# Moving the steps of a softmax in a fused FFT and mixture-of-experts kernel: normalisation, transposition and input rounding

## The chip, the cores and the metric

The kernel runs on one core of one Trainium2 chip. The metric is the device time of one execution in microseconds (us). An execution of the kernel before took 1669.15 us in the median of three (1666.14 to 1671.22).

## The reference

The input is x with 8 batches of 3072 x 256. What is computed, cut to what matters:

```
X = fft(fft(x, axis=1), axis=2).real          # 8 x 3072 x 256, then 24576 rows of 256
x = (X @ w_a * (X @ w_b)) @ w_out             # 256 -> 1536 -> 256
logits = x @ phi                              # 24576 x 32
d = softmax of logits over the 24576 rows     # one column for each of 32 slots
slot_input = d.T @ x                          # 32 x 256, 8 experts of 4 slots
slot_out = per expert relu(slot_input @ w1) @ w2
c = softmax of logits over the 32 slots       # one row for each of 24576 rows
out = c @ slot_out
```

All of it is single precision. Both softmaxes subtract the maximum, and add 1e-9 to the sum that they divide by.

## The kernel before, in words

**Three stages.** `_fft` makes the transform in the first 214 us of the profiled execution. `_main` runs the loop over 24 blocks of rows, three for each batch, and ends with `tail`, which computes the slots. `_out` writes the result in the last 65 us.

**The loop.** A block k has 12 steps p, one for each 128 of the 1536 hidden columns (n = 12 k + p). The order of each engine's instructions is the order in which the program writes them; nothing reorders them. In a step:

- `layer1(n)`: TensorE makes 12 products of 512 columns into four PSUM tiles s0, s1, d0, d1, each of one buffer. VectorE adds and subtracts them (L547 twice, then L552, L553, L554), ScalarE copies d1 (L551, `db`), and GpSimd makes the products `g` of the two layers with three instructions that read and write SBUF (L556, L557, L558). In every third block (k % 3 = 2) GpSimd also copies one column (L561). The next step's s products can't start before L547 has read s, nor its d products before L552, L553 and L554 have read d.
- `transp(n - 2)`: eight transpositions of `g` by TensorE (L579) and a copy of them by ScalarE into a ring (L582).
- at p = 1, 5 and 9: `logits` of four steps (L590, 32 products).
- `run_side(k - 1, ...)`: the softmax of the block before, by the list `side`, and with p = 5, 9 and the next block's 1 the product `z_part` (L599, 16 products) with its sum into `acc` (L602).

**The softmax of a block** has the parts `l` and `m` (p = 1: copy of the logits, maximum, exponential `dt` L620), `d` (p = 3), `ct` (p = 4, transposition), `cm` (row maximum L643, subtraction L644, exponential L645), `sum` (the sum of `dt`, L625, and the running sum L626), `cs` (the normalisation: sum L650 on VectorE, plus eps L651 on ScalarE, reciprocal L652 and product L653 on VectorE) and `co` (two transpositions L658, copy L660, store to DRAM by SyncE's queue L661). The list before is

```
side = {3: ["d"], 4: ["ct"], 5: ["cm", "sum", 0], 9: ["cs", 1], 10: ["co"]}
```

**The next block's inputs** are loaded by `load_eo(k + 1)`, written at p = 1, into one buffer `eoraw`. `split_eo(k + 1)` at p = 9, written right behind `layer1`, rounds them to `eoh` on ScalarE (L516) and takes the rest `eol` as a difference on VectorE (L519), an instruction with two inputs in SBUF. Both tiles have two buffers.

Of the kernel before, what the change touches and what calls it, by code (L numbers as in the profile page):

```python
# [10 lines left out]
F32R = mybir.dt.float32r  # L11
U32 = mybir.dt.uint32
U64 = mybir.dt.uint64
ACTF = mybir.ActivationFunctionType
ALU = mybir.AluOpType
AX = mybir.AxisListType
# [3 lines left out]
P = 128  # L20
# [467 lines left out]
def _main(tc, ctx, wtp, wt, w128, outs, eo, wsc, exu, ident, m_sb, ex_e, csc, nblk, wof, w1, w2):  # L488
    nc = tc.nc
    nb = nblk // 3  # L490
    ep = ctx.enter_context(tc.tile_pool(reuse_waits="tile", name="m_e", bufs=2))
    eh = ctx.enter_context(tc.tile_pool(reuse_waits="tile", name="m_h", bufs=2))
# [9 lines left out]
    eo_t = {}  # L502

    def load_eo(k):
        raw = ep.tile([P, 2, 512], F32, tag="eoraw", name="eoraw", bufs=1)
        ub = ep.tile([P, 512], F32, tag="ub", name="ub")
        nc.sync.dma_start(raw, eo[k])
        nc.sync.dma_start(ub, eo[k][0:1, 1, :].to_broadcast([P, 512]))
        eo_t[k] = [raw, ub]

    def split_eo(k):
        raw, ub = eo_t[k]
        l = eh.tile([P, 2, 512], F32R, tag="eol", name="eol")
        h = eh.tile([P, 2, 512], F32R, tag="eoh", name="eoh")
        if k:
            nc.scalar.copy(h, raw)  # L516
        else:
            nc.vector.tensor_copy(h, raw)
        nc.vector.tensor_tensor(l, raw, h.bitcast(F32), ALU.subtract)  # L519
        eo_t[k] = (h, l, ub)  # L520

    load_eo(0)
    split_eo(0)
    nper = nblk * NFT
    g_t = {}
    r_t = {}
# [57 lines left out]
    def logits(n):  # L584
        k, ft = divmod(n, NFT)
        g = g_t[n] if n == nper - 1 else g_t.pop(n)
        if ft == 0:
            l_ps[k] = ps.tile([P, 256], F32, tag="l", name="l_ps")
        for c in range(4):
            nc.tensor.matmul(l_ps[k][NS * c:NS * c + NS], m_sb[:, ft], g[:, 256 * c:256 * c + 256],  # L590
                             start=(ft == 0), stop=(ft == NFT - 1))

    def z_part(k, q, tag="x"):
        z_ps = ps.tile([P, 512], F32, tag=tag, name="z_ps")
        d_sb, alpha = soft[k]["d"], soft[k]["alpha"]
        ring = r_t.pop((k, q))
        for hh in range(2):
            for c in range(4):
                nc.tensor.matmul(z_ps[NS * c:NS * c + NS], d_sb[:, hh, NS * c:NS * c + NS],  # L599
                                 ring[:, :, 2 * c + hh, :], start=(hh == 0), stop=(hh == 1))  # L600
        sl = acc[:, q * 512:q * 512 + 512]
        nc.vector.scalar_tensor_tensor(out=sl, in0=sl, scalar=alpha, in1=z_ps,  # L602
                                       op0=ALU.mult, op1=ALU.add)

    def soft_step(k, step):
        s = soft.setdefault(k, {})
        if step == "l":
            l_sb = p2.tile([P, 256], F32, tag="l_sb", bufs=1, name="l_sb")
            (nc.scalar.copy if k < nblk - 1 else nc.vector.tensor_copy)(l_sb, l_ps.pop(k))
            s["l"] = l_sb  # L610
        elif step == "m":
            l_sb = s["l"]
            m_old, m_new = m_run[k % 2], m_run[1 - k % 2]
            bm = p2.tile([P, 4], F32, tag="sm", name="sm")
            dt_ = p2.tile([P, 256], F32, tag="dt", bufs=1, name="dt")
            nc.vector.tensor_reduce(out=bm[:, 0:1], in_=l_sb, axis=AX.X, op=ALU.max)
            nc.vector.tensor_tensor(m_new, bm[:, 0:1], m_old, ALU.max)
            nc.vector.tensor_scalar_mul(bm[:, 1:2], m_new, -1.0)
            al = p2.tile([P, 2], F32, tag="al", name="al")
            nc.scalar.activation(dt_, l_sb, ACTF.Exp, bias=bm[:, 1:2])  # L620
            nc.scalar.activation(al[:, 0:1], m_old, ACTF.Exp, bias=bm[:, 1:2])
            s["dt"], s["alpha"], s["al"] = dt_, al[:, 0:1], al
        elif step == "sum":
            al = s["al"]
            nc.vector.tensor_reduce(out=al[:, 1:2], in_=s["dt"], axis=AX.X, op=ALU.add)  # L625
            nc.scalar.activation(l_run, l_run, ACTF.Identity, scale=al[:, 0:1], bias=al[:, 1:2])  # L626
        elif step == "d":
            y_ps = ps.tile([P, 2, P], F32, tag="x", name="y_ps")
            for hh in range(2):
                nc.tensor.transpose(y_ps[:, hh], s["dt"][:, hh * P:hh * P + P], ident)  # L630
            d_sb = p2.tile([P, 2, P], F32, tag="d_sb", bufs=1, name="d_sb")
            nc.scalar.copy(d_sb, y_ps)
            s["d"] = d_sb
        elif step == "ct":
            x_ps = ps.tile([P, 4, P], F32, tag="x", name="x_ps")
            for hh in range(2):
                nc.tensor.transpose(x_ps[:, hh], s["l"][:, hh * P:hh * P + P], ident)
            s["xl"] = x_ps
        elif step == "cm":
            x_ps = s.pop("xl")[:, 0:2].rearrange("p h (c s) -> p (h c) s", c=4)  # L640
            cm = p1.tile([P, 8], F32, tag="cm", name="cm")
            ce = p1.tile([P, 8, NS], F32, tag="ce", name="ce")
            nc.vector.tensor_reduce(out=cm, in_=x_ps, axis=AX.X, op=ALU.max)  # L643
            nc.vector.tensor_tensor(ce, x_ps, cm.unsqueeze(2).to_broadcast([P, 8, NS]), ALU.subtract)  # L644
            nc.scalar.activation(ce, ce, ACTF.Exp)  # L645
            s["ce"] = ce
        elif step == "cs":
            ce = s["ce"]
            cs = p1.tile([P, 8], F32, tag="cs", name="cs")
            nc.vector.tensor_reduce(out=cs, in_=ce, axis=AX.X, op=ALU.add)  # L650
            nc.scalar.activation(cs, cs, ACTF.Identity, bias=eps)  # L651
            nc.vector.reciprocal(out=cs, in_=cs)  # L652
            nc.vector.tensor_tensor(ce, ce, cs.unsqueeze(2).to_broadcast([P, 8, NS]), ALU.mult)  # L653
        elif step == "co":
            x_ps = ps.tile([P, 2, P], F32, tag="x", name="c_ps")
            cf = s["ce"].rearrange("p a s -> p (a s)")
            for hh in range(2):
                nc.tensor.transpose(x_ps[:, hh], cf[:, hh * P:hh * P + P], ident)  # L658
            ct = p2.tile([P, 256], F32, tag="ct", bufs=1, name="ct")
            nc.scalar.copy(ct, x_ps.rearrange("p h t -> p (h t)"))  # L660
            nc.sync.dma_start(csc[:, k], ct)  # L661

    side = {3: ["d"], 4: ["ct"], 5: ["cm", "sum", 0], 9: ["cs", 1], 10: ["co"]}

    def run_side(k, items):
        for v in items:
            if isinstance(v, str):
                soft_step(k, v)
            else:
                z_part(k, v)  # L670

    ex = {}
# [62 lines left out]
    def tail(k, rest):  # L735
        load_w1(2)
        soft_step(k, "m")
        rest()
        soft_step(k, "sum")
        load_w2(0)  # L740
        soft_step(k, "d")
# [120 lines left out]
    for z in range(4):  # L862
        nc.vector.tensor_reduce(out=fold[:, z], in_=ident.rearrange("p (c s) -> p s c", c=4),
                                axis=AX.X, op=ALU.add)
# [4 lines left out]
    for n in range(nper + 2):  # L869
        k, p = divmod(n, NFT)  # L870
        if n < nper:
            if p == 1 and k + 1 < nblk:
                load_eo(k + 1)
            layer1(n)
            if p == 9 and k + 1 < nblk:
                split_eo(k + 1)
            if n < 9:
                extra(n)
            if n == NFT:
                nc.sync.dma_start(wo, wof)  # L880
        if n == nper + 1:
            for z in range(5, 1, -1):
                logits(n - z)
        if n >= 2:
            rest = transp(n - 2)
        if n == nper:
            z_part(nblk - 2, 2)
        if n % 4 == 1 and 1 < n < nper:
            for z in range(5, 1, -1):
                logits(n - z)  # L890
        if k > 0 and p == 1:
            soft_step(k - 1, "l")
            if n < nper:
                soft_step(k - 1, "m")
                if k > 1:
                    z_part(k - 2, 2)
        if k > 0 and n < nper:
            run_side(k - 1, side.get(p, []))
        if k == nblk - 1 and p in ahead:
            ahead[p]()  # L900
# [40 lines left out]
def _build(tc, x, x384, w_a, w_b, w_out, phi, w1, w2, tabs, fdft, out):  # L941
# [3 lines left out]
    with ExitStack() as ctx, tc.manual_schedule():  # L945
# [45 lines left out]
        with ExitStack() as c1:  # L991
            cin, first, so_h, so_l = _main(tc, c1, wtp, wt, w128, outs, eo, wsc, exu, ident, m_sb, ex_e, csc,
                                    nblk, wof, w1, w2)
# [36 lines left out]
```

## Time and profile before

| | us |
|---|---|
| three executions: lowest, median, highest | 1666.14, 1669.15, 1671.22 |
| the profiled execution | 1664.62 |
| its span, from the first to the last instruction | 1662.6 |
| busy in the span: TensorE (PE) | 1598.5 (96%) |
| VectorE (DVE) | 1391.2 (84%) |
| GpSimd (POOL) | 1146.9 (69%) |
| ScalarE (ACT) | 640.8 (39%) |
| mean granted clock of TensorE | 0.98 of its upper level |

The profiled execution is a run of its own, 4.5 us below the median. PE, DVE, ACT and POOL are the engines' names in the profile; PEld is TensorE's weight load and SPq SyncE's queue of transfers. Matmuls overlap, so that the time from the start of one to the start of the next is a better measure than its duration.

### The profile page before, as it was taken

To read this page: it belongs to the slowest core of one execution; us is meant where nothing else is said; L and a number is where in the kernel's file an instruction comes from. 1 tells how busy PE (TensorE), PEld (TensorE's weight loads), DVE (VectorE), ACT (ScalarE), POOL (GpSimd) and SP (SyncE) were. 2 spreads that over 40 slices of the span, in tenths; PEclk is the share of its full clock that TensorE was granted. 3 is DMA by queue.
4 is the path that set the end of the run, shared out by engine and by line. 5 is a ranking of instruction groups with operands and counts; after the bars stand their busy time and mean duration, and the time that the engine had idled before them with its cause. 6 is when DMAs were issued, how large, how long until landed. Compare 5 with 4: busy or idle time off the path is not lost.

```text
span 1662.6 us, 28294 instructions
## 1 busy us (share of the span) xinstructions
PE 1598.5 (96%) x10837; PEld 1166.9 (70%) x10837; DVE 1391.2 (84%) x2055; ACT 640.8 (39%) x990; POOL 1146.9 (69%) x992
## 2 busy tenths in 40 slices
PE   5999999999999999999999999999999999999985
PEld 3555578777777777777777777777777777777554
DVE  8999889888888888888888988888888888888633
ACT  1322324434434444434343443433443434434343
POOL 1000069888878887888788778877887788878421
PEclk9999999999999999999999999999999999999975
DMA  9777330000000000000000000000000000002689
GB/s 392 271 249 243 106 98 20 23 1 23 24 23 1 23 23 23 1 23 23 23 1 23 23 20 4 23 23 16 8 23 23 1 23 23 23 1 94 281 338 385
DMA packets 34095, 123.71 MB, mean 74 GB/s; under 512 B 3780, under 2 KB 12035, under 8 KB 26792
## 3 DMA queue, kind: packets, MB, share of 16 engines
q1 hardware_dynamic: 28796, 113.98, 18.7%
q10 hardware_dynamic: 5164, 7.92, 1.3%
q8 instruction: 86, 1.41, 0.4%
q14 instruction: 49, 0.40, 0.1%
HBM read 79.36 MB, written 42.52 MB: 73 GB/s over the span
## 4 chain that ended last, share of the span: by engine, by line
PE 81%; DVE 11%; DMA 4%; issue 2%; ACT 1%; POOL 0%; DVEq 0%; ACTq 0%; SPq 0%
PE t_ps L579 14%; PE s L531 8%; PE d L531 8%; PE d L533 8%; PE d L532 8%; PE s L533 7%; PE s L532 7%; PE l_ps L590 7%; PE z_ps L599 6%; PE pt L262 4%; DMA out_dram<-o 3%; DVE eol L519 2%; PE pt L171 1%; DVE f L269 1%; DVE e L276 1%
## 5 line engine op out<-in xcount | busy, mean ns | idle before, releaser
L556 POOL TENSOR_TENSOR db<-s_sb,db 128x512 f32<-128x512 f32 x287 | 373.0, 1300 | 249.7 <-DVE s_sb L553 99.1
L547 DVE SCALAR_TENSOR_TENSOR s_sb<-ub,w,s 128x512 f32<-128x512 f32 x576 | 404.4, 743 | 72.0 <-PE s L533 69.8
L551 ACT COPY db<-d 128x512 f32<-128x512 f32 x288 | 169.7, 589 | 626.7 <-PE d L533 608.7
L557 POOL TENSOR_TENSOR g<-pl 128x512 f32<-128x512 f32 x288 | 384.9, 1336 | 7.7 <-DVE pl L554 6.9
L558 POOL TENSOR_TENSOR g<-s_sb,db 128x512 f32<-128x512 f32 x287 | 372.4, 1298 | 0.0
L582 ACT COPY ring<-t_ps 128x1024 f32<-128x1024 f32 x286 | 290.5, 1016 | 63.8 <-PE t_ps L579 63.8
L579 PE MATMUL t_ps<-ident,g 128*128 128x128 f32 x2296 | 297.3, 272 | 0.0
L579 PEld LDWEIGHTS t_ps<-ident,g 128*128 128x128 f32 x2296 | 268.3, 140 | 39.3 <-issue 0.4
L531 PE MATMUL s<-eoh,wt 128*128 128x512 f32 x576 | 252.6, 438 | 2.4 <-DVE s_sb L547 2.4
L531 PE MATMUL d<-eoh,wt 128*128 128x512 f32 x576 | 226.9, 394 | 3.1 <-DVE s_sb L553 3.1
L533 PE MATMUL d<-eoh,wt 128*128 128x512 f32 x576 | 227.2, 394 | 0.0
L533 PE MATMUL s<-eoh,wt 128*128 128x512 f32 x576 | 226.5, 393 | 0.0
L532 PE MATMUL s<-eol,wt 128*128 128x512 f32 x576 | 225.2, 391 | 0.0
L532 PE MATMUL d<-eol,wt 128*128 128x512 f32 x576 | 225.1, 391 | 0.0
L553 DVE TENSOR_TENSOR s_sb<-s_sb,d 128x512 f32<-128x512 f32 x288 | 197.8, 687 | 9.9
L554 DVE TENSOR_TENSOR pl<-s_sb,d 128x512 f32<-128x512 f32 x288 | 197.5, 686 | 0.5 <-ACT db L551 0.5
L552 DVE TENSOR_TENSOR pl<-s_sb,d 128x512 f32<-128x512 f32 x288 | 195.6, 679 | 0.0
L531 PEld LDWEIGHTS s<-eoh,wt 128*128 128x128 f32 x576 | 108.4, 188 | 76.1 <-issue 28.9
L590 PE MATMUL l_ps<-g,m_sb 128*32 128x256 f32 x2304 | 139.2, 382 | 0.0
L599 PE MATMUL z_ps<-ring,d_sb 128*32 128x512 f32 x1152 | 136.7, 592 | 0.0
L531 PEld LDWEIGHTS d<-eoh,wt 128*128 128x128 f32 x576 | 108.2, 188 | 30.7 <-DVE s_sb L553 7.6
L533 PEld LDWEIGHTS s<-eoh,wt 128*128 128x128 f32 x576 | 108.1, 188 | 25.0
(186 smaller groups left out, 1699.5 us busy)
## 6 DMA issues: line engine op xcount, KB each, us to landing
out_dram<-o SPq DMA_DIRECT2D x23, 1024.0 KB
xt<-in_x_dram SPq DMA_DIRECT2D x15, 1536.0 KB
eoraw<-eo_c SPq DMA_DIRECT2D x16, 512.0 KB
w2t<-in_moe_w_dram SPq DMA_DIRECT2D x4, 2048.0 KB
w1t<-in_moe_w_dram SPq DMA_DIRECT2D x3, 2048.0 KB
eo<-so SPq DMA_DIRECT2D x16, 256.0 KB
eoraw<-eo SPq DMA_DIRECT2D x8, 512.0 KB
ub<-eo_c SPq DMA_DIRECT2D x16, 256.0 KB
```

The costliest lines, as they stand in the source:

```text
L531: nc.tensor.matmul(ps_, wt[ft // 4][:, ft % 4, 0, e, ab], h[:, e], start=True, stop=False)
L532: nc.tensor.matmul(ps_, wt[ft // 4][:, ft % 4, 0, e, ab], l[:, e], start=False, stop=False)
L533: nc.tensor.matmul(ps_, wt[ft // 4][:, ft % 4, 1, e, ab], h[:, e], start=False, stop=True)
L547: nc.vector.scalar_tensor_tensor(out=s_sb[:, ab], in0=ub, scalar=w128[:, ab, ft:ft + 1], in1=s_ps[ab], op0=ALU.mult, op1=ALU.add)
L553: nc.vector.tensor_tensor(am, s_sb[:, 0], d_ps[0], ALU.subtract)
L556: eng.tensor_tensor(bm, s_sb[:, 1], db, ALU.subtract)
L557: nc.gpsimd.tensor_tensor(g[:, 0:512], pl[:, 0], pl[:, 1], ALU.mult)
L558: eng.tensor_tensor(g[:, 512:1024], am, bm, ALU.mult)
L579: nc.tensor.transpose(t_ps[:, z], g[:, z * P:z * P + P], ident)
L582: nc.scalar.copy(dst, t_ps)
L590: nc.tensor.matmul(l_ps[k][NS * c:NS * c + NS], m_sb[:, ft], g[:, 256 * c:256 * c + 256], start=(ft == 0), stop=(ft == NFT - 1))
L599: nc.tensor.matmul(z_ps[NS * c:NS * c + NS], d_sb[:, hh, NS * c:NS * c + NS], ring[:, :, 2 * c + hh, :], start=(hh == 0), stop=(hh == 1))
```

## The change

`split_eo` becomes two functions, `split_h` (the rounding) and `split_l` (the difference), which `run_side` calls at p = 8 and p = 9, behind the step's transpositions. The normalisation `cs` goes from p = 9 to p = 5, behind `sum` and ahead of the first `z_part`, and `co` from p = 10 to p = 7. The reduction L625 is taken out: the exponential L620 gives its sum by `accum_out`. `run_side` is now called in block 0 too, for the two new steps alone.

```diff
-    def split_eo(k):
-        raw, ub = eo_t[k]
+    def split_h(k):
+        h = eh.tile([P, 2, 512], F32R, tag="eoh", name="eoh")
+        (nc.scalar.copy if k else nc.vector.tensor_copy)(h, eo_t[k][0])
+        eo_t[k].append(h)
+
+    def split_l(k):
+        raw, ub, h = eo_t[k]
         l = eh.tile([P, 2, 512], F32R, tag="eol", name="eol")
-        h = eh.tile([P, 2, 512], F32R, tag="eoh", name="eoh")
-        if k:
-            nc.scalar.copy(h, raw)
-        else:
-            nc.vector.tensor_copy(h, raw)
         nc.vector.tensor_tensor(l, raw, h.bitcast(F32), ALU.subtract)
         eo_t[k] = (h, l, ub)
 
     load_eo(0)
-    split_eo(0)
+    split_h(0)
+    split_l(0)
...
-            nc.scalar.activation(dt_, l_sb, ACTF.Exp, bias=bm[:, 1:2])
+            nc.scalar.activation(dt_, l_sb, ACTF.Exp, bias=bm[:, 1:2], accum_out=al[:, 1:2])
...
             al = s["al"]
-            nc.vector.tensor_reduce(out=al[:, 1:2], in_=s["dt"], axis=AX.X, op=ALU.add)
...
-    side = {3: ["d"], 4: ["ct"], 5: ["cm", "sum", 0], 9: ["cs", 1], 10: ["co"]}
+    side = {3: ["d"], 4: ["ct"], 5: ["cm", "sum", "cs", 0], 7: ["co"], 8: ["h"], 9: ["l", 1]}
 
     def run_side(k, items):
+
         for v in items:
-            if isinstance(v, str):
+            if v in ("h", "l"):
+                if k + 2 < nblk:
+                    (split_h if v == "h" else split_l)(k + 2)
+            elif k >= 0 and isinstance(v, str):
                 soft_step(k, v)
-            else:
+            elif k >= 0:
                 z_part(k, v)
...
             layer1(n)
-            if p == 9 and k + 1 < nblk:
-                split_eo(k + 1)
...
-        if k > 0 and n < nper:
+        if n < nper:
             run_side(k - 1, side.get(p, []))
```

## Rows read from the trace of the kernel before

**Rows 1.** Windows, the loop: length, busy and count by engine, PEclk, DMA.
```profile
215.00:1556.00 1341.00, 1335.48 (x9281) 1007.08 (x9281) 1148.17 (x1755) 540.92 (x785) 1115.80 (x956) 1.00 0.07 23
```

**Rows 2.** Timeline, PE, steps 10 and 11 at 1100 us: start, us, instruction [idle before it].
```profile
1099.92 0.50 PE L531 MATMUL s<-eoh,wt 128*128 128x512 f32 x1
...
1103.65 0.38 PE L658 MATMUL c_ps<-ident,ce 128*128 128x128 f32 x2
...
1105.26 0.39 PE L531 MATMUL d<-eoh,wt 128*128 128x512 f32 x1
...
1107.43 0.48 PE L531 MATMUL s<-eoh,wt 128*128 128x512 f32 x1
```

**Rows 3.** Timeline, PE, the same steps of the block at 923 us.
```profile
930.86 0.50 PE L531 MATMUL s<-eoh,wt 128*128 128x512 f32 x1
...
935.21 0.50 PE L531 MATMUL s<-eoh,wt 128*128 128x512 f32 x1 [0.22 <-DVE s_sb L547]
...
937.19 0.50 PE L531 MATMUL d<-eoh,wt 128*128 128x512 f32 x1 [0.31 <-DVE s_sb L553]
...
939.49 0.47 PE L531 MATMUL s<-eoh,wt 128*128 128x512 f32 x1
```

**Rows 4.** Timeline, DVE, that block; in brackets the idle time and its end.
```profile
928.14 4.35 DVE L519 TENSOR_TENSOR eol<-eoraw,eoh 128x1024 fp32r<-128x1024 f32 x1 [0.26 <-ACT eoh L516]
932.40 0.41 DVE L650 TENSOR_REDUCE cs<-ce 128x8 f32<-128x256 f32 x1
...
933.42 0.43 DVE L653 TENSOR_TENSOR ce<-ce,cs 128x256 f32<-128x256 f32 x1
933.76 0.74 DVE L602 SCALAR_TENSOR_TENSOR acc<-acc,al,z_ps 128x512 f32<-128x512 f32 x1
934.42 1.40 DVE L547 SCALAR_TENSOR_TENSOR s_sb<-ub,w,s 128x512 f32<-128x512 f32 x2
...
936.45 0.69 DVE L553 TENSOR_TENSOR s_sb<-s_sb,d 128x512 f32<-128x512 f32 x1
```

**Rows 5.** Timeline, POOL, that block: the last instruction of step 9's run.
```profile
930.07 1.33 POOL L558 TENSOR_TENSOR g<-s_sb,db 128x512 f32<-128x512 f32 x1
```

**Rows 6.** Windows, L519 alone, two blocks: window, length, busy, PEclk, DMA.
```profile
418.40:430.20 11.80, 4.34 (x1) 1.00 0.01 2
...
1317.20:1329.00 11.80, 4.32 (x1) 1.00 0.01 1
```

**Rows 7.** Timeline, DVE, step 5: a block with L561, and one without.
```profile
857.07 0.75 DVE L602 SCALAR_TENSOR_TENSOR acc<-acc,al,z_ps 128x512 f32<-128x512 f32 x1 [2.00 <-PE z_ps L599]
...
909.93 0.42 DVE L644 TENSOR_TENSOR ce<-x_ps,cm 128x256 f32<-128x256 f32 x1
...
912.68 0.75 DVE L602 SCALAR_TENSOR_TENSOR acc<-acc,al,z_ps 128x512 f32<-128x512 f32 x1 [2.00 <-PE z_ps L599]
```

**Rows 8.** Timeline, POOL, the last L558 of step 5 in these two blocks.
```profile
856.43 1.29 POOL L558 TENSOR_TENSOR g<-s_sb,db 128x512 f32<-128x512 f32 x1
...
911.41 1.27 POOL L558 TENSOR_TENSOR g<-s_sb,db 128x512 f32<-128x512 f32 x1
```

**Rows 9.** Timeline, ACT: db of step 2, the exponential of step 5, db of step 9.
```profile
896.93 0.59 ACT L551 COPY db<-d 128x512 f32<-128x512 f32 x1 [2.62 <-PE d L533]
...
910.39 0.42 ACT L645 ACTIVATE ce<-ce 128x256 f32<-128x256 f32 x1 [0.31 <-DVE ce L644]
...
926.57 0.59 ACT L551 COPY db<-d 128x512 f32<-128x512 f32 x1 [1.81 <-PE d L533]
```

**Rows 10.** Timeline, SyncE's queue: the load behind the csc store.
```profile
936.87 0.32 SPq L507 DMA_DIRECT2D eoraw<-eo_c  x1
```

**Rows 11.** Timeline, PE, the tail: transposition of the running sum.
```profile
1563.67 0.27 PE L747 MATMUL mp<-ident,l_run 128*1 128x128 f32 x1 [0.82 <-ACT l_run L626]
```

**Rows 12.** Timeline, DVE and POOL, step 9 of a block with L561.
```profile
871.24 1.30 POOL L558 TENSOR_TENSOR g<-s_sb,db 128x512 f32<-128x512 f32 x1
...
872.53 1.22 DVE L519 TENSOR_TENSOR eol<-eoraw,eoh 128x1024 fp32r<-128x1024 f32 x1 [0.26 <-ACT eoh L516]
```

## The prediction

> **What bounds the kernel now.** I read the windows first: over the loop PE is busy for 1335.5 of 1341.0 us at its upper clock level, 1.00 [rows 1]. So nothing that only shortens VectorE, ScalarE or GpSimd is worth time, unless PE waits for it. Since matmuls overlap, a busy sum does not tell lost time: I then read PE's timeline from start to start, step by step through all blocks. All blocks from the third on run alike, except at one place. From the first s product of step 10 to the first of the step after 11, it takes 1107.43 - 1099.92 = 7.51 us in one block [rows 2] and 939.49 - 930.86 = 8.63 us in another [rows 3]. In the second, PE has two short waits, for L547 ahead of s and for L553 ahead of d: VectorE is late in giving PSUM back. The loss is 8.63 - 7.51 = 1.12 us, much more than the two idle times beside the rows, 0.22 and 0.31, which start only where the modelled ends of the matmuls stop.
>
> VectorE's timeline shows why [rows 4]. L519 takes 4.35 us at 928.14 and ends at 932.49. GpSimd's three instructions of the step run back to back until 930.07 + 1.33 = 931.40 [rows 5], and L519 ends 1.09 us after that: it has stood still and worked only then. Behind it stand the normalisation (L650 at 932.40 to L653 at 933.42, 1.36 us until L602 can start at 933.76), L602, and only then L547 of step 10 at 934.42.
>
> The windows of L519 alone by block say how often [rows 6]: 23 windows, of which 9 read 4.31 to 4.35 us (the first at 418, the last at 1317 us), 7 read 1.22 or 1.23 (each a block with L561), and 7 read 1.82 to 2.04, where VectorE came in between two GpSimd instructions. Exactly the 9 are the blocks that lose time. So 9 x 1.12 = 10.1 us of the execution are VectorE's lateness at step 10, and I find no other repeated loss in the loop.
>
> The rule that bears on it: the Trainium skill, SBUF — State Buffer, section "SBUF: two separate sides", says that VectorE and GpSimd share one pair of SBUF ports under an exclusive lock, that a VectorE operation with two SBUF inputs needs it against a GpSimd operation that reads SBUF, and that whoever starts first keeps it for its instruction. The trace agrees on who blocks whom. By the rule L519 would wait for one GpSimd instruction, no block would lose, and this change would give nothing (1664.6). The rows show it passed over by more than one, and the measurement decides.
>
> **The change part by part.** *Normalisation away from step 9.* Behind L519 stands only L602 then. In the block of [rows 4] it starts at 932.40 instead of 933.76 and everything behind it comes 1.36 us sooner: L547 at 933.06, L553 ends at 936.45 + 0.69 - 1.36 = 935.78. When does PE want d of step 11? In the block without loss 1105.26 - 1099.92 = 5.34 us after step 10's start, and up to 0.38 less because the two transpositions L658 leave step 10 [rows 2]: 930.86 + 5.34 = 936.20, or 935.82 at the earliest [rows 3]. VectorE is done 0.04 to 0.42 us ahead. The cover is thin but it holds, so the 9 losses go: -10.1 us, even where L519 still waits for three GpSimd instructions. Bounds: nothing regained if what is late is L519 itself, all of it if the sum above holds; I take all of it.
>
> *Normalisation in step 5.* L644 ends at 910.35; L645 on ScalarE ends at 910.81 [rows 9]; the way from L650 to L653 took 933.42 - 932.40 = 1.02 us [rows 4], so L653 can start at about 911.9 and L602 0.34 later. L602 starts at 912.68 today after 2.00 us of idling for PE's z product [rows 7]: the chain fits into that idle time, which the removed L625 widens. But L653 has two SBUF inputs, and GpSimd runs until 911.41 + 1.27 = 912.68 [rows 8]. At worst it starts then, and L602 0.34 us late. In blocks with L561 GpSimd ends at 856.43 + 1.29 = 857.72, and L602 would start at 858.06 instead of 857.07 [rows 7, 8], 0.99 late. What is allowed: from L602 to L553's end are 936.45 + 0.69 - 933.76 = 3.38 us [rows 4], PE wants d 5.34 - 0.38 = 4.96 us after step 6's start at the earliest [rows 2], and L602 starts now about when that step does: some 1.5 us are free. Cost nothing; the cover is that distance. GpSimd has no more work until the next step's db, so it can't pass L653 over twice.
>
> *Transposition and store in step 7.* The same two transpositions and the same copy, moved by three steps; L653 has ended by far. The store L661 moves forward in SyncE's queue, where the next load of eoraw stands behind it today at 936.87 [rows 10] and then waits for L519 alone; it is used a block later. In the last block a load of expert weights goes behind the store by about a step; its reader is in the tail. Cost nothing.
>
> *Rounding in step 8.* Behind the step's ring copy ScalarE idles for 1.81 us ahead of db of step 9 [rows 9], and the rounding fits in: today it runs behind that db, and L519, which waits for it, starts at 928.14, so that db and rounding together take 928.14 - 926.57 = 1.57 us, the rounding alone about 1.0 [rows 4, 9]. Cost nothing; without the cover about 1 us in 23 blocks, which would delay db and with it GpSimd, not PE at once. L519 no longer waits 0.26 us for it [rows 4, 12], but then waits for GpSimd.
>
> *Sum from the accumulator.* No row shows such an instruction. From below: nothing. From above: one more ScalarE instruction as long as the exponential L645, 0.42 us [rows 9]. At step 1 ScalarE idles for 2.62 us ahead of the next db [rows 9]: nothing. In the tail the running sum is on the path (PE's transposition waits for L626) [rows 11], so 0 to 0.42 us, once; I take 0.3, since reading one sum should be nearer to an instruction than to nothing. L625 was on no path: nothing is gained by its going.
>
> **The sum.** The profiled execution took 1664.6 us (span 1662.6 and 2.0 around it): 1664.6 - 10.1 + 0.3 = 1654.8. The median of the runs is 4.5 above the profiled execution. Which blocks lose is a toss between two engines, and the 7 that read 1.82 to 2.04 could lose as well (7 x 1.12 = 7.8 us), so part of that distance, and of the 5.1 us between the runs, may be the same loss and go too. If all of it goes, the median is 1654.8, if none, 1659.3. I forecast 1656, nearer to the first.
>
> **The rivals.**
> *A. As above:* 1656, of its own 1653 to 1660. Chance 0.64.
> *B. GpSimd wins in the blocks with L561.* There L519 asks at 872.53, as L558 ends (871.24 + 1.30 = 872.54), and gets through [rows 12]. Now it asks 0.26 earlier, while L558 runs. If GpSimd goes on through L561 and three more instructions, its run ends 0.26 + 3 x 1.3, about 4.2 us, after the asking, against 931.40 - 927.88 = 3.5 in [rows 4, 5]: 0.6 to 0.7 later, with 0.04 to 0.42 to spare. That costs 0.2 to 0.6 us in 7 blocks, up to 4.2: 1657.5 to 1660. For it: nine blocks were passed over. Against it: a request so near to an instruction's end came through in every one of these 7 blocks. Chance 0.13. By the rule of the Trainium skill cited above, L519 gets its turn at L558's end and this loses nothing.
> *C. The change doesn't do what it says:* L519's 4.35 us alone are enough, because the spare 0.04 to 0.42 us is overdrawn. Half of the loss stays: 1661; all: 1668. Against it: 1.36 us less stand behind L519. Chance 0.13, mostly at the far end.
> *D. The chain in step 5 becomes the new stall:* L653 kept out for longer than 1.5 us beyond today's L602 start. Each tenth over that costs 2.2 us in 22 blocks; three tenths make 1663. Against it: GpSimd is idle by then [rows 8]. Chance 0.05.
> *E. Slower:* the exponential with a sum takes ScalarE far longer than a small instruction. It decides from where it eats the 2.62 us ahead of step 2's db [rows 9] and then 10.1 / 23 = 0.44 us more: 3.1 us on top of L620, in 23 blocks. At 3.5 us the time would be 1656 + 23 x 0.88 = 1676. Against it: a whole exponential over the same 256 columns, L645, takes 0.42 [rows 9]. Chance 0.05.
>
> **How the numbers follow.** About 0.3%, 5 us here, can be told from no change: faster means under 1664.1, slower over 1674.2. A, B, D and 0.03 of C are faster: 0.85. The rest of C is the same: 0.10. E is slower: 0.05. The range runs from 1652 (A with all the distance to the median regained, and 3 us for the spread of the runs) to 1664, so that A, B, D and the near part of C lie inside.
>
> **What would show it.** After the change PE's timeline should read about 7.3 us from step 10's start to the start of the step after 11, in every block, with no wait for L547 or L553, although some windows of L519 still read over 4 us. L653 should lie between L645 and L602 in step 5, and L602 there should idle for well under 2.00 us. ScalarE's db of step 9 should follow its rounding without delay. The prediction is wrong if PE still waits at step 11, or newly at step 7 or step 2; B is seen by L519 over 4 us in blocks with L561.

## The result, and the profile after

| | us |
|---|---|
| changed kernel, four executions: lowest, median, highest | 1652.9, 1654.68, 1658.54 |
| kernel before beside it, four executions | 1666.14, 1669.64, 1671.22 |
| ratio, 95% interval | 0.9917 (0.9903 to 0.9932) |
| profiled execution after (before) | 1654.5 (1664.6) |
| its span | 1652.5 (1662.6) |

The kernel is 0.8% faster; the forecast was 1656 in 1652 to 1664. The sum, made against the profiled execution, was 1654.8, and the profiled execution after took 1654.5. In the order in which the prediction reads the profile:

**The loop**, from its first s product to the last step's. First the changed kernel's window, then the kernel before's, which was not shown (length, then busy time and count of PE, PEld, DVE, ACT, POOL, then PEclk and DMA):

```profile
215.40:1541.00 1325.60, 1325.22 (x9257) 1004.36 (x9257) 1128.73 (x1723) 542.59 (x806) 1118.61 (x953) 1.00 0.07 23
```
```profile
215.50:1552.80 1337.30, 1331.78 (x9257) 1003.83 (x9257) 1144.79 (x1750) 539.64 (x782) 1112.68 (x953) 1.00 0.07 23
```

The loop is 1337.30 - 1325.60 = 11.7 us shorter.

**Steps 10 and 11.** PE's timeline of the changed kernel from step 10 to the start of the step after 11, in answer to [rows 2, 3]:

```profile
925.29 0.50 PE L532 MATMUL s<-eoh,wt 128*128 128x512 f32 x1
...
928.94 0.47 PE L532 MATMUL s<-eoh,wt 128*128 128x512 f32 x1
...
930.40 0.39 PE L532 MATMUL d<-eoh,wt 128*128 128x512 f32 x1
...
932.57 0.47 PE L532 MATMUL s<-eoh,wt 128*128 128x512 f32 x1
```

932.57 - 925.29 = 7.28 us, and no wait stands in brackets. All blocks from the second on read 7.28 or 7.29. Against the blocks without loss before, 7.51 - 7.28 = 0.23 us of this is no gain: the two transpositions L658 now stand in step 7, which takes 3.85 us instead of 3.63. VectorE in that block, in answer to [rows 4] (L547, L553 and L602 are one line lower now, L548, L554 and L603), then GpSimd, in answer to [rows 5]:

```profile
922.22 1.97 DVE L519 TENSOR_TENSOR eol<-eoraw,eoh 128x1024 fp32r<-128x1024 f32 x1
925.42 0.75 DVE L603 SCALAR_TENSOR_TENSOR acc<-acc,al,z_ps 128x512 f32<-128x512 f32 x1 [1.23 <-PE z_ps L600]
926.36 1.41 DVE L548 SCALAR_TENSOR_TENSOR s_sb<-ub,w,s 128x512 f32<-128x512 f32 x2 [0.19 <-PE s L534]
```
```profile
921.80 1.30 POOL L557 TENSOR_TENSOR db<-s_sb,db 128x512 f32<-128x512 f32 x1
923.05 2.27 POOL L558 TENSOR_TENSOR g<-pl 128x512 f32<-128x512 f32 x1
925.28 1.29 POOL L559 TENSOR_TENSOR g<-s_sb,db 128x512 f32<-128x512 f32 x1
```

Here is what I had not foreseen: L519 does not wait for three instructions any more. It gets in behind the first, and now it is GpSimd that stands still: its second instruction reads 2.27 us instead of 1.30. VectorE then idles for 1.23 us until PE's z product. Over all blocks L519's longest is 2.10 us. So the loss is gone, but not, in this execution, by the way that I had reckoned (a long wait with nothing behind it). The experiments have to tell what did it.

Step 5 in the same block, VectorE, in answer to [rows 7]:

```profile
904.15 0.42 DVE L644 TENSOR_TENSOR ce<-x_ps,cm 128x256 f32<-128x256 f32 x1
905.06 0.42 DVE L650 TENSOR_REDUCE cs<-ce 128x8 f32<-128x256 f32 x1 [0.48 <-ACT ce L645]
905.85 0.20 DVE L652 RECIPROCAL cs<-cs 128x8 f32<-128x8 f32 x1 [0.37 <-ACT cs L651]
906.08 1.10 DVE L653 TENSOR_TENSOR ce<-ce,cs 128x256 f32<-128x256 f32 x1
907.11 0.73 DVE L603 SCALAR_TENSOR_TENSOR acc<-acc,al,z_ps 128x512 f32<-128x512 f32 x1
```

L653 waits for GpSimd's last instruction (1.10 us instead of 0.43), and L603 starts 907.11 - 904.15 = 2.96 us after L644, against 912.68 - 909.93 = 2.75 before [rows 7]: 0.21 late, for free. In the block with L561 at 847 us it got in ahead of GpSimd's last instruction (0.50 us), and L603 still idled 0.32 us for z: the 0.99 that was feared there did not come. ScalarE at steps 8 and 9, in answer to [rows 9], and the new instruction, as the table of groups has it (count, busy us, mean ns):

```profile
919.09 1.05 ACT L513 CAST eoh<-eoraw 128x1024 fp32r<-128x1024 f32 x1
920.99 0.59 ACT L552 COPY db<-d 128x512 f32<-128x512 f32 x1 [0.85 <-PE d L534]
```
```profile
L621 ACT ACTIVATION_READ_ACCUMULATOR dt<-l_sb,sm 128x1 f32 x24 | 4.5, 186 | 0.0
```

The rounding lies in ScalarE's idle time with 0.85 us to spare, and the sum costs a reading instruction of 186 ns beside the exponential, whose own time stays 510 ns.

**The tail** (all that follows the loop) gave 1.7 us back: from the last step on it took 1652.5 - 1541.0 = 111.5 us, against 1662.6 - 1552.8 = 109.8 before. Windows of the changed kernel:

```profile
1546.00:1552.30 6.30, 4.49 (x60) 2.28 (x51) 3.35 (x7) 2.23 (x6) 2.35 (x4) 1.00 1.00 417
1552.30:1555.70 3.40, 3.40 (x20) 0.84 (x24) 0.64 (x2) 0.67 (x2) 0.00 (x0) 0.50 0.99 417
```

From 1552.3 to 1555.7 us PE's granted clock is 0.50, the lower level, after a stretch in which it was busy for 4.49 of 6.30 us. Before, the stretch that answers to it reads 1.00:

```profile
1563.90:1567.50 3.60, 3.60 (x34) 0.94 (x33) 2.12 (x7) 0.67 (x2) 0.00 (x0) 1.00 0.99 414
```

### The profile page after: what moved, and what is told of

It reads as the page before. It is cut to its first block, busy times and chain, and to the rows that moved or that the text cites. A ratio compares the mean times of both kernels' runs of the same rounds, so it can differ in the third digit from the quotient of the medians.

```text
span 1652.5 us, 28244 instructions
## 1 busy us (share of the span) xinstructions
PE 1594.0 (96%) x10837; PEld 1167.8 (71%) x10837; DVE 1375.4 (83%) x2031; ACT 643.9 (39%) x1014; POOL 1151.3 (70%) x992
## 4 chain that ended last, share of the span: by engine, by line
PE 88%; DVE 6%; DMA 3%; issue 1%; ACT 0%; POOL 0%; DVEq 0%; ACTq 0%; SPq 0%
PE t_ps L580 15%; PE s L532 9%; PE l_ps L591 8%; PE d L534 8%; PE s L534 8%; PE s L533 8%; PE d L533 8%; PE d L532 8%; PE z_ps L600 8%; PE pt L262 4%; DMA out_dram<-o 2%; PE pt L171 1%; DVE f L269 1%; DVE e L276 1%; DVE dz L284 1%
## 5 line engine op out<-in xcount | busy, mean ns | idle before, releaser
L548 DVE SCALAR_TENSOR_TENSOR s_sb<-ub,w,s 128x512 f32<-128x512 f32 x576 | 404.6, 744 | 80.2 <-PE s L534 76.2
L558 POOL TENSOR_TENSOR g<-pl 128x512 f32<-128x512 f32 x288 | 392.0, 1361 | 1.3 <-DVE pl L555 1.0
L554 DVE TENSOR_TENSOR s_sb<-s_sb,d 128x512 f32<-128x512 f32 x288 | 197.8, 687 | 9.9
L553 DVE TENSOR_TENSOR pl<-s_sb,d 128x512 f32<-128x512 f32 x288 | 195.5, 679 | 0.0
L532 PEld LDWEIGHTS s<-eoh,wt 128*128 128x128 f32 x576 | 108.5, 188 | 70.7 <-issue 39.8
L533 PEld LDWEIGHTS d<-eol,wt 128*128 128x128 f32 x576 | 108.2, 188 | 24.3
```

Source lines behind the costliest of these rows:

```text
L532: nc.tensor.matmul(ps_, wt[ft // 4][:, ft % 4, 0, e, ab], h[:, e], start=True, stop=False)
L533: nc.tensor.matmul(ps_, wt[ft // 4][:, ft % 4, 0, e, ab], l[:, e], start=False, stop=False)
L548: nc.vector.scalar_tensor_tensor(out=s_sb[:, ab], in0=ub, scalar=w128[:, ab, ft:ft + 1], in1=s_ps[ab], op0=ALU.mult, op1=ALU.add)
L558: nc.gpsimd.tensor_tensor(g[:, 0:512], pl[:, 0], pl[:, 1], ALU.mult)
```

## The experiments

**Theory 1** is the prediction's: VectorE is late because a chain stands behind L519, and PE loses what VectorE is late beyond a room, the time by which VectorE may be late without PE having to wait. **Theory 2** came from the profile after: the change works because L519 asks for its ports earlier and gets in between two GpSimd instructions.

### The kernel before once more

> The kernel before, unchanged, profiled once more. If the number of blocks in which L519 waits for three GpSimd instructions differs from execution to execution and is what spreads the times, the profiled time is about 1654.5 + 1.12 us for each such block (9 blocks made 1664.6): with 13 blocks 1669. If the number is fixed and the spread comes from elsewhere, it is 9 again, whatever the time.

Measured: 1665.68 us, with 10 blocks of 4.31 us and more, seven of the nine of the first profile and three others. The number changes from execution to execution. The loop is 1338.25 - 1337.30 = 0.95 us longer than in the first profile, about what one block more loses. That 1654.5 + 10 x 1.12 = 1665.7 hits the time is luck: 1654.5 is the changed kernel's time, and its loop and tail also differ by other amounts, which nearly cancel.

### Each part alone

First the normalisation, which takes its transposition and store along to step 7.

```diff
-side = {3: ["d"], 4: ["ct"], 5: ["cm", "sum", 0], 9: ["cs", 1], 10: ["co"]}
+side = {3: ["d"], 4: ["ct"], 5: ["cm", "sum", "cs", 0], 7: ["co"], 9: [1]}
```

> Only the normalisation goes to step 5 and its transposition to step 7; the rounding stays at step 9, so that L519 asks for its ports at the old moment. Theory 1 (the work behind L519 makes VectorE late): some windows of L519 still read over 4 us, yet steps 10 and 11 take 7.3 us in every block, and the time is that of the changed kernel, about 1655, ratio 0.991. Theory 2 (the change works because L519 asks 0.26 us earlier and gets in between two GpSimd instructions): the waits over 4 us stay and most of the loss with them, 1664 to 1669, ratio 0.997 to 1.000.

Measured: 1654.84 us, ratio 0.9931 (0.9911 to 0.9952): the whole gain. Steps 10 and 11 take 7.28 us in every block from the second on. Then the rounding alone:

```diff
-side = {3: ["d"], 4: ["ct"], 5: ["cm", "sum", 0], 9: ["cs", 1], 10: ["co"]}
+side = {3: ["d"], 4: ["ct"], 5: ["cm", "sum", 0], 8: ["h"], 9: ["l", "cs", 1], 10: ["co"]}
...
-            if p == 9 and k + 1 < nblk:
-                split_eo(k + 1)
```

> Only the rounding goes to step 8, and L519 behind the transpositions of step 9, still ahead of the normalisation, which stays at step 9. Theory 1 alone: the chain of 1.36 us still stands behind L519, so with waits over 4 us in about 9 blocks the time is that of before, 1664 to 1669. Theory 2: no window of L519 over 4 us, steps 10 and 11 take 7.5 us in every block, about 1655, ratio 0.991, although the chain still stands behind it.

Measured: 1665.68 us, ratio 1.0000 (0.9988 to 1.0012): nothing. L519 asks about 0.3 us earlier here and still waits for more than 4 us in 10 blocks, and each of them loses time. One line on L519 for these two runs (shortest, median and longest ns), first the normalisation alone, then the rounding alone:

```profile
L519 DVE TENSOR_TENSOR eol<-eoraw,eoh x24: 1224/1639/2365, 214.5 to 1479.6; 128x1024 fp32r<-128x1024 f32 x24
```
```profile
L519 DVE TENSOR_TENSOR eol<-eoraw,eoh x24: 1218/2162/4671, 213.5 to 1489.6; 128x1024 fp32r<-128x1024 f32 x24
```

And the timeline of VectorE in one of the blocks that lose in the second:

```profile
927.85 4.67 DVE L519 TENSOR_TENSOR eol<-eoraw,eoh 128x1024 fp32r<-128x1024 f32 x1
932.44 0.41 DVE L651 TENSOR_REDUCE cs<-ce 128x8 f32<-128x256 f32 x1
...
934.45 1.40 DVE L548 SCALAR_TENSOR_TENSOR s_sb<-ub,w,s 128x512 f32<-128x512 f32 x2
```

It is [rows 4] again: the earlier asking only makes the wait longer, it ends at the same place. Theory 2 falls. But theory 1 is not shown by these two either, since with the normalisation moved the long waits were gone too. The third part, the sum:

```diff
-nc.scalar.activation(dt_, l_sb, ACTF.Exp, bias=bm[:, 1:2])
+nc.scalar.activation(dt_, l_sb, ACTF.Exp, bias=bm[:, 1:2], accum_out=al[:, 1:2])
...
-nc.vector.tensor_reduce(out=al[:, 1:2], in_=s["dt"], axis=AX.X, op=ALU.add)
```

> Only the sum from the accumulator. Both theories: no change beyond the spread, ratio 0.997 to 1.003; 0.19 us more on ScalarE at step 1, hidden in the loop, and about 0.1 to 0.2 us once in the tail.

Measured: ratio 0.9995 (0.9981 to 1.0009). No change, as both theories said; 9 long waits.

### Long waits without the chain

```diff
+        if k:
+            tick = p1.tile([P, 1], F32, tag="tick", name="tick")
+            nc.vector.tensor_scalar_mul(tick, eps, -1.0)
         nc.vector.tensor_tensor(l, raw, h.bitcast(F32), ALU.subtract)
```

> The changed kernel with one small VectorE instruction (128 x 1, about 0.15 us) ahead of L519, so that it asks for its ports about 0.75 us instead of 0.89 us before the end of GpSimd's L557, the place at which the kernel before was refused in about half of its blocks. If the moment of asking decides, windows over 4 us come back in some blocks. Theory 1 (only what stands behind L519 costs time): even then steps 10 and 11 take 7.3 us in every block and the time is that of the changed kernel, ratio 0.991 to 0.994. Rival (L519's wait by itself makes the loss): each such block loses about 1 us, with 10 of them ratio 0.997 to 1.000.

Measured: 1659.53 us, ratio 0.9933 (0.9916 to 0.9949). That is 5 us above the changed kernel, but none of it lies at steps 10 and 11: in the profile the clock is at 0.50 for two stretches of the tail, of 3.4 and some 10 us. Two blocks had long waits, of 4.40 and 4.41 us, the others 2.02 us at most. One of the two, VectorE, then PE:

```profile
923.28 4.41 DVE L522 TENSOR_TENSOR eol<-eoraw,eoh 128x1024 fp32r<-128x1024 f32 x1
927.61 0.74 DVE L606 SCALAR_TENSOR_TENSOR acc<-acc,al,z_ps 128x512 f32<-128x512 f32 x1
928.27 1.40 DVE L551 SCALAR_TENSOR_TENSOR s_sb<-ub,w,s 128x512 f32<-128x512 f32 x2
```
```profile
926.29 0.50 PE L535 MATMUL s<-eoh,wt 128*128 128x512 f32 x1
...
933.57 0.48 PE L535 MATMUL s<-eoh,wt 128*128 128x512 f32 x1
```

A wait of 4.41 us, and 933.57 - 926.29 = 7.28: no loss. This is theory 1's step itself. A few waits came back, not half of them, so that the moment of asking is not shown to decide who gets in. Nor did the run hit the moment that it was meant to: L519 asked 0.81 to 0.86 us before the end of GpSimd's instruction, where the kernel before had asked 0.74 to 0.79 us before it.

### How much room there is

```diff
         nc.vector.tensor_tensor(l, raw, h.bitcast(F32), ALU.subtract)
         eo_t[k] = (h, l, ub)
+        if k:
+            for _ in range(2):
+                pad = p1.tile([P, 1], F32, tag="pad", name="pad")
+                nc.vector.tensor_reduce(out=pad, in_=h.bitcast(F32).rearrange("p a f -> p (a f)"),
+                                        axis=AX.X, op=ALU.max)
```

The other run has `range(3)`.

> The changed kernel with two reductions over eoh, 2.3 to 2.5 us in all, on VectorE between L519 and L602 in step 9: VectorE is as late as if L519 had waited over 4 us in every block. Theory 1 gives 2.8 us of room there (L602 may start up to 926.97 where it starts at 925.42 now, and L519 ends at 924.19): steps 10 and 11 take 7.3 us, time as the changed kernel, at most 0.3 us a block more. Rival: a wait of that length is the loss, about 1 us in 22 or 23 blocks, 1676 to 1680.

Measured: 1658.81 us (profiled 1662.17), ratio 0.9936 (0.9919 to 0.9953). Where L519 is short, two reductions (2.46 us) cost nothing from the second block on (7.27 to 7.28 us; the first, whose step 9 has no z product, loses 1.1). L519 waited long in 4 blocks; there both delays meet. VectorE and PE in one of these:

```profile
1149.74 4.45 DVE L519 TENSOR_TENSOR eol<-eoraw,eoh 128x1024 fp32r<-128x1024 f32 x1
1154.12 2.46 DVE L524 TENSOR_REDUCE pad<-eoh 128x1 f32<-128x1024 f32 x2
1156.49 0.74 DVE L608 SCALAR_TENSOR_TENSOR acc<-acc,al,z_ps 128x512 f32<-128x512 f32 x1
```
```profile
1152.81 0.50 PE L537 MATMUL s<-eoh,wt 128*128 128x512 f32 x1
...
1157.94 0.50 PE L537 MATMUL s<-eoh,wt 128*128 128x512 f32 x1 [1.23 <-DVE s_sb L553]
...
1162.22 0.47 PE L537 MATMUL s<-eoh,wt 128*128 128x512 f32 x1
```

The two steps take 1162.22 - 1152.81 = 9.41 us: 2.13 lost. Four times that and the first block's 1.1 make the time longer than the changed kernel's, which was not expected, since the waits had not been.

> The same with three reductions, 3.4 to 3.7 us: L519's wait and the normalisation's 1.36 us in every block. Theory 1: past the room by 0.7 to 0.9 us, so steps 10 and 11 take about 8.0 to 8.3 us in every block and the time is 16 to 21 us over the changed kernel, near 1673. Rival as for two reductions: more than that by another 1.2 us a block.

Measured: 1677.65 us (profiled 1676.3), ratio 1.0043 (1.0020 to 1.0065), a little above what was expected. Without a long wait, VectorE and PE:

```profile
933.13 3.71 DVE L524 TENSOR_REDUCE pad<-eoh 128x1 f32<-128x1024 f32 x3
936.76 0.74 DVE L608 SCALAR_TENSOR_TENSOR acc<-acc,al,z_ps 128x512 f32<-128x512 f32 x1
```
```profile
934.29 0.50 PE L537 MATMUL s<-eoh,wt 128*128 128x512 f32 x1
...
940.19 0.50 PE L537 MATMUL d<-eoh,wt 128*128 128x512 f32 x1 [0.30 <-DVE s_sb L559]
...
942.49 0.48 PE L537 MATMUL s<-eoh,wt 128*128 128x512 f32 x1
```

942.49 - 934.29 = 8.20 us, 0.92 lost, with a wait for d alone, as theory 1 says. Now the law can be read, with x as the start of the sum into `acc` after the first s product of step 10, and the loss over 7.28:

| | x | lost | x - lost |
|---|---|---|---|
| three reductions | 936.76 - 934.29 = 2.47 | 0.92 | 1.55 |
| two reductions and a long wait | 1156.49 - 1152.81 = 3.68 | 2.13 | 1.55 |
| kernel before, long wait and normalisation [rows 3, 4] | 933.76 - 930.86 = 2.90 | 1.12 over 7.51 | 1.78 |
| later asking, long wait | 927.61 - 926.29 = 1.32 | 0 | |

What VectorE is late beyond 1.55 us is lost one for one. In the kernel before, the two transpositions in step 10 give 7.51 - 7.28 = 0.23 more room, which makes the same 1.55. Work and wait count alike. In the blocks with L561 the three reductions make x 1.71 and lose 0.13 us, which fits too.

One block does not fit: with three reductions and a long wait together x is 4.93 us, and 4.44 us are lost instead of 3.38. There PE waited 2.48 us, and behind that wait its granted clock read 0.50 from 1278.9 to 1282.3 us, with its products 0.43 us apart instead of 0.23:

```profile
1277.94 0.50 PE L537 MATMUL s<-eoh,wt 128*128 128x512 f32 x1 [2.48 <-DVE s_sb L553]
```

So the law is shown as far as x = 3.68, where PE waited 1.23 us and the clock stayed at 1.00.

### The same work in another order

```diff
-side = {3: ["d"], 4: ["ct"], 5: ["cm", "sum", 0], 8: ["h"], 9: ["l", "cs", 1], 10: ["co"]}
+side = {3: ["d"], 4: ["ct"], 5: ["cm", "sum", 0], 8: ["h"], 9: ["cs", 1, "l"], 10: ["co"]}
```

The diff is against the run with the rounding alone.

> The normalisation stays at step 9, but L519 goes behind it and behind L602, where GpSimd's run of the step is over or nearly so; the rounding is at step 8. All the work of step 9 before the change is still there, only in another order. Theory 1 (GpSimd's run ahead of a chain): L519 takes 1.2 to 1.6 us, VectorE is in time, steps 10 and 11 take 7.5 us in every block, ratio 0.991 to 0.994. Rival (the normalisation at step 9 is too much work there): the loss stays, ratio 0.998 to 1.002.

Measured: 1654.72 us, ratio 0.9909 (0.9895 to 0.9924): the whole gain, with the normalisation left at step 9 and all of VectorE's work still there. VectorE in one block:

```profile
923.79 2.78 DVE L654 TENSOR_TENSOR ce<-ce,cs 128x256 f32<-128x256 f32 x1
926.50 0.73 DVE L603 SCALAR_TENSOR_TENSOR acc<-acc,al,z_ps 128x512 f32<-128x512 f32 x1
927.16 1.21 DVE L519 TENSOR_TENSOR eol<-eoraw,eoh 128x1024 fp32r<-128x1024 f32 x1
```

The normalisation's product now takes the wait for GpSimd (2.78 instead of 0.43), but most of it lies in the time in which VectorE would idle for z: the sum into `acc` starts 0.7 us after step 10's first s product instead of 0.14, well inside the room. L519 then reads 1.2 us (1.7 in the blocks with L561). Steps 10 and 11 take at most 0.07 us more than 7.52. So the normalisation at step 9 is not too much work; it stood in the wrong place.

### The changed kernel again, and its tail

> The changed kernel once more, beside the next two on the same chip. Its loop is the same every time (no loss at steps 10 and 11), so its times differ from run to run only by the stages before and behind the loop: in its first profile TensorE's granted clock stood at 0.50 from 1552.3 to 1555.7 us, in the tail, and the tail was 1.8 us longer than in the kernel before. Expected 1655, ratio 0.990 to 0.994.

Measured: 1655.04 us, ratio 0.9927 (0.9915 to 0.9940), and in this execution one long wait, in the changed kernel itself:

```profile
811.24 4.45 DVE L519 TENSOR_TENSOR eol<-eoraw,eoh 128x1024 fp32r<-128x1024 f32 x1
815.61 0.73 DVE L603 SCALAR_TENSOR_TENSOR acc<-acc,al,z_ps 128x512 f32<-128x512 f32 x1
```
```profile
814.31 0.50 PE L532 MATMUL s<-eoh,wt 128*128 128x512 f32 x1
...
821.59 0.48 PE L532 MATMUL s<-eoh,wt 128*128 128x512 f32 x1
```

821.59 - 814.31 = 7.28: harmless, as predicted. The clock fell in the tail at the same place as in the first profile. Then the changed kernel with transpositions that nothing uses, in PE's two pauses there:

```diff
+        keep = ps.tile([P, 4, P], F32, tag="d0", name="keep")
+        for z in range(8):
+            nc.tensor.transpose(keep[:, z % 4], ident, ident)
         soft_step(k, "d")
...
         nc.tensor.transpose(mp[:, 0], m_run[nblk % 2], ident)
+        for z in range(7):
+            nc.tensor.transpose(keep[:, z % 4], ident, ident)
         nc.tensor.transpose(mp[:, 1], l_run, ident)
```

> The changed kernel with 15 transpositions of the identity, used by nothing, in the two pauses of TensorE in the tail (8 ahead of the softmax's transposition y_ps, 7 ahead of that of the running sum). If the pauses bring the lower clock level that follows them, the clock stays at 1.00 until the output stage, and the tail has 43.1 us from the last step on instead of 44.9: 1.8 us less in the profile, ratio lower by 0.001 to 0.002 than the changed kernel's. If the fall has another cause, nothing changes, or 0.1 to 0.3 us are lost because the transpositions come too late to fit.

Measured: 1654.52 us, ratio 0.9918 (0.9904 to 0.9932). The window that read 0.50 before:

```profile
1552.30:1555.70 3.40, 3.34 (x31) 1.70 (x35) 0.64 (x2) 2.18 (x6) 0.00 (x0) 1.00 1.01 429
```

The clock stays at 1.00 until the output stage. In time it is 0.5 us in the median, which the intervals don't separate from the changed kernel. Nor is it shown that the transpositions kept the clock up: the run with two reductions has the changed kernel's tail without them, with the same pauses of 0.99 and 0.82 us, and reads 1.00 behind them as well:

```profile
1561.70:1565.10 3.40, 3.40 (x32) 0.86 (x32) 2.05 (x6) 0.67 (x2) 0.00 (x0) 1.00 0.99 416
```

The last run has the same transpositions, with L519 last as above.

> The normalisation at step 9 ahead of L519, as in the run with L519 last, and the 15 transpositions in the tail. Against that run (profile 1652.7, no fall of the clock in the tail) nothing is to be gained by them: 1654 to 1656, ratio 0.990 to 0.993. If it is below the changed kernel with the same transpositions, the order with L519 last is the better one by itself.

Measured: 1655.63 us, ratio 0.9928 (0.9916 to 0.9941), not better than the changed kernel with or without the transpositions. I find no version that is clearly faster than the changed kernel.

## Why the prediction was right, and where it was not

**The bound and the place** were right: apart from the first blocks PE loses time at steps 10 and 11 alone, through VectorE's lateness, and the loss is gone in all blocks.

**Normalisation away from step 9** was right, and with its transposition it is the whole gain (0.9931 alone, against 0.9995 and 1.0000 for the other parts). The room had been put at 4.96 - 3.38 = 1.58 us at the least and is 1.55. The step "even where L519 still waits for three GpSimd instructions" held in the three blocks in which it could be seen without other work behind it (4.40 to 4.45 us, no loss). But the prediction expected such waits in some blocks of every execution, and they nearly vanished: 9, 10 and 9 blocks in the three profiles that have the kernel before's step 9, none and one in the two of the changed kernel. So most blocks gain by the work behind L519 and by its shorter wait at once. Why GpSimd lets VectorE in more often stays open; the earlier asking alone does not do it.

**Two transpositions in step 7** had been booked at nothing, but seem to have widened the cover, and that is luck. By the prediction's own figures the sum into `acc` would start 932.40 - 930.86 = 1.54 us after step 10's first s product, which leaves 0.01 of the room of 1.55. Measured in the blocks with a long wait it is 1.30 to 1.32, because GpSimd's run of step 9 now starts 925.29 - 921.80 = 3.49 us ahead of step 10, where it started 930.86 - 927.60 = 3.26 ahead of it:

```profile
927.60 1.33 POOL L556 TENSOR_TENSOR db<-s_sb,db 128x512 f32<-128x512 f32 x1
```

Outside the blocks with L561, every run with the transpositions in step 7 reads 3.45 to 3.50 from the second block on, and every run that has them in step 10 and L519 ahead of the normalisation 3.24 to 3.31. This shift against GpSimd's run, and not the normalisation, may also be what makes the long waits rare (8 of 105 such blocks, against 38 of 60); no run moves one without the other.

**The size.** 9 x 1.12 = 10.1 us was forecast and the loop gave 11.7. The nine blocks lost about 1.1 us each at steps 10 and 11, 9.8 in all. Another 0.8 lies in the first block, where VectorE's first rounding now runs ahead of a wait for PE instead of behind it (at 209.62 instead of 213.63 us), so that PE no longer waits 0.48 us for L547 in the loop's second step; the prediction had not seen that. The rest is hundredths at other steps. The tail took 1.7 back by its clock, which the prediction had not in its sum; that the two misses nearly cancel is luck. The sum from the accumulator was put at 0.3 in the tail: the reading instruction is 0.19, and the pause ahead of the softmax's transposition grew by 0.99 - 0.90 = 0.09.

**Steps 5, 7 and 8** cost PE nothing beyond the two transpositions' own time, as forecast, and at step 5 by the bound that was named: L653 waits for GpSimd's last instruction.

**The distance between the runs.** I had put part of the 4.5 us between the median and the profiled execution down to the number of long waits. That number does change, but the three profiles have 9 or 10, which is 1 us. The rest comes from outside the loop, as far as the profiles show: in the three of the changed kernel's loop (first profile, again, with transpositions in the tail) the time from its first s product to the last step's is 1324.9 us each time. Over all 13 profiles the stage ahead of the loop takes 214 to 217 us, and from the last step's start to PE's product `rp`, behind the experts, it is 41.9 to 42.1 us where the clock stays up and 43.5 to 47.7 where it falls.

**The rivals.** B (GpSimd wins in the blocks with L561) did not come: in every block with L561 L519 reads 1.2 to 1.4 us in the changed kernel and in the run with the rounding alone, where it asks earlier. C (L519's wait alone is enough) is refuted by the harmless long waits, with 1.55 - 1.32 = 0.23 us to spare. D (the chain in step 5 as the new stall) did not come. E (a slow exponential) is refuted by the 186 ns.

## What to carry to other kernels

When an engine is late at one step, measure how late it may be there, and count waits and work behind each other alike: here moving 1.36 us of work out of the way, or only putting it in front of the operation that waits, took the whole loss away; where the work was moved and the long wait came all the same (three blocks), nothing was lost. An operation that competes for a shared resource belongs where the other engine's run has ended, or ahead of idle time, not ahead of a chain. And the stage behind a loop can run at another clock from one execution to the next (0.50 for 3.4 us here): look at the granted clock of the tail before adding up.

## What the runs showed of the hardware

VectorE's operation with two SBUF inputs can wait for three GpSimd instructions in a row (4.1 to 4.7 us instead of 1.2), and when it gets in, GpSimd's next instruction reads 2.27 us instead of 1.30. The Trainium skill, SBUF — State Buffer, section "SBUF: two separate sides", has the lock and who holds it, which these rows bear out; that the one which asked first may lose to the other's next instruction is this case's measurement, not the page's. Which of the two wins at an instruction's end differed between blocks whose timelines agree to hundredths: in the kernel before L519 read 1.83 us in a block in which it asked 0.75 us before that end, and 4.32 us in another in which it asked 0.76 us before it.

PE's clock went to 0.50 for 3.4 us in the tail, right after two pauses of 0.99 and 0.82 us, in both profiles of the changed kernel and in the runs with later asking and with three reductions. In the runs with two reductions and with the sum alone the same two pauses were not followed by a fall, so that the pauses are not enough by themselves. From the last step's start to PE's product `rp` it took 43.8 us in both profiles of the changed kernel, against 42.1 in the run with two reductions, which has the same tail at the upper level: the fall costs 1.7 us there. What brings it about stays open.
